# Seven half-size output products in three chunks of batches two and three

## The chip, the core and the metric

The kernel runs on one core of a Trainium2 chip. Its time is the device time of one execution in microseconds: before the change the median of three runs is 566.68 us, the lowest 566.61 and the highest 567.18. The profile is of one further execution, whose span is 564.8 us; times inside it count from the start of that span. TensorE (PE) multiplies matrices, VectorE (DVE) and ScalarE (ACT) work elementwise, GpSimd (POOL) issues the loads, and SyncE (SP) issues the stores and the transposing transfers. The clock granted to PE was full through the whole profile.

## The reference

Four batches of cross-covariance attention are followed by a feed-forward with a product of two projections. The attention matrix is 256 by 256 per batch, and it is made from sums over all 5824 rows; no nonlinear step follows the first product.

```python
def _attn_ref(q, k, v, tau):                         # q, k, v: (4, 5824, 256)
    qn = q / (np.linalg.norm(q, axis=1, keepdims=True) + 1e-06)
    kn = k / (np.linalg.norm(k, axis=1, keepdims=True) + 1e-06)
    s = kn.transpose(0, 2, 1) @ qn / tau             # (4, 256, 256)
    s = s - s.max(-1, keepdims=True)
    a = np.exp(s)
    a /= a.sum(-1, keepdims=True) + 1e-09
    return (v @ a).astype(np.float32)

def _moe_ref(x, w1, w2, w3, w_out):                  # x: (23296, 256), w1, w2: (256, 1024)
    a = x @ w1
    b = x @ w2
    h = a * b @ w3                                   # w3: (1024, 1024)
    return (h @ w_out).astype(np.float32)            # w_out: (1024, 256)
```

## The kernel before

The kernel never forms the attention output. It folds each batch's 256 by 256 attention matrix into the two projection weights (Wf), and it multiplies w3 by w_out once (W_sb). What is left per row is two projections of v, their elementwise product, and one output product of 1024 by 256.

A batch is cut into 12 chunks of rows: eleven of 512 rows and a last one of 192 columns (128 rows, and the 64 left over, which are handled for two batches together). A chunk has eight slots, one for each 128 of the 1024 features. A slot is the unit of the schedule: it makes the two projections into two PSUM banks, lets ACT cast the first to SBUF, and lets DVE multiply it by the second, straight from PSUM. There are four such banks, used in turn, so that a bank is wanted again two slots later. The evictions of the folds use the same four.

```python
    def bank(tag):
        if tag == "out":
            return {"tag": "out", "bufs": 3}
        turns[0] += 1
        return {"tag": f"ab{turns[0] % 4}", "bufs": 1}

    def emit_ab(b, c, j):
        n = chunk_cols(c)
        tiles = []
        for w in range(2):
            t = psum.tile([P, 512], F32, name=f"{'ab'[w]}_{b}_{c}_{j}", **bank("ab"))
            for ct in range(CT):
                nc.tensor.matmul(t[:, :n], lhsT=Wf[b][:, ct, w, j * P : (j + 1) * P], rhs=rhs_of(b, c, ct),
                                 start=(ct == 0), stop=(ct == CT - 1))
            tiles.append(t)
        a_sb = work.tile([P, 512], BF16, tag="a_sb", name=f"as_{b}_{c}_{j}", bufs=4)
        nc.scalar.copy(a_sb[:, :n], tiles[0][:, :n])
        # ... the last chunk: the same into left, with 192 columns
            ab = halves[j // 4][:, j % 4, :]
            nc.vector.tensor_mul(ab, a_sb, tiles[1])
        # ...
        if not seven(b, c):
            pend.append((slot[0] + LAG, 1, lambda only=None: emit_out(b, c, j, ab, only)))
        elif j == FT - 1:
            fns = seven_products(b, c, *halves)
            fns[0]()
            pend.extend((slot[0] + 1, 2, fn) for fn in fns[1:])
```

The output of a plain chunk is four matmuls of 256 columns in each slot (`emit_out`), two slots behind the projections, and two copies of 512 columns at the end, one on ACT and one on DVE. In batch four, and only there, the chunks but the last two take another way: the output product of the chunk, seen as 2 by 2 blocks, is made of seven products of half size and not of eight. That costs four sums on DVE for the left sides (s1 to s4), seven products of eight matmuls with 128 columns each, four copies of 256 columns on ACT and three additions of 256 columns on DVE. The right sides are prepared once, from W_sb, at the start of batch two (`combine_weights`: four differences on DVE and two casts on ACT). The seven products need the whole chunk, so that they are made in the slots of the next one, one product in each slot.

```python
    def seven(b, c):
        return b == B - 1 and c < NCH - 2

        # in seven_products:
        def p1():
            st["o"] = work.tile([P, 4, D], F32, tag="o_sb", name=f"osb_{b}_{c}", bufs=3)
            nc.vector.tensor_sub(s2, s1, a11)
            product("A", a11, w1, True)
            keep(0, 0)                               # ACT copies A to SBUF
        def p5():
            nc.vector.tensor_sub(s3, a11, a21)
            product("C", s1, t1, True)
        def p6():
            product("A", s2, t2)                     # adds onto A in the same bank
            keep(0, 1)
        # ... p7, p2, p4, p3 in the same manner
        return [sum1, p1, p5, p6, p7, p2, p4, p3]
```

While a batch runs, the scores of the next are made in the gaps: for each pair of rows, a G pair of matmuls and a square on ACT for the first row with q and another for the second with k, then one addition of the squares on DVE (1024 columns in fp32). After the scores comes a chain (norms, exponentials, sums), and then eight folds. All of this is placed by an agenda: each entry has a time on a clock that the emission of matmuls advances.

```python
        units = score_units(n)                       # 23 pairs x 3 units
        for i, (cst, fn) in enumerate(units):
            at(t0 + (t1 - t0) * i / len(units), cst, fn)      # t0, t1 = 16.0, 98.0 in batches two and three
        soft = soft_units(n)
        for cst, t, fn in soft:
            at(t1 + 1.0 + t, cst, fn)                # t: 0 (norms) ... 14.6 (sums), 15.6 + 1.1 * i (fold i)
    # ...
    for b in range(B):
        make_agenda(b)
        for c in range(NCH):
            for j in range(FT):
                run_due()
                emit_ab(b, c, j)
                room = 2
                while w_ready[0] and len(pend) > lag and pend[0][0] <= slot[0] and pend[0][1] <= room:
                    _, size, fn = pend.pop(0)
                    fn()
                    room -= size
                    run_due()
        run_due(1e9)
```

A plain output matmul group has size 1 and one of the seven products size 2, so that a slot holds at most two groups or one product.

Of the kernel before, what the change touches and what calls it, by code (L numbers as in the profile page):

```python
# [13 lines left out]
BF16 = DT.bfloat16  # L14

P = 128
# [9 lines left out]
def kernel(  # L26
# [12 lines left out]
    nc = tc.nc  # L39

    B, N, C = q.shape
# [9 lines left out]
    FT = F // P  # L51
# [6 lines left out]
    NCH = NT // 4 + 1  # L58
# [9 lines left out]
    work = ctx.enter_context(tc.tile_pool(name="work", bufs=2))  # L68
# [111 lines left out]
    def score_units(n):  # L180

        units = []
        npair = (NT + 1) // 2

        def pair_unit(pr, part):
            i0 = 2 * pr
            pi, o = divmod(i0, PIECE)
            qt, kt = pieces["q", n, pi], pieces["k", n, pi]
            if pr == 0 and part == 0:
                G_tiles[n] = psum.tile([P, CT, C], F32, tag="G", name=f"G_{n}", bufs=1)  # L190
                accs[n] = work.tile([P, 2, 2, C], F32, tag="acc", name=f"acc_{n}", bufs=1)
            G = G_tiles[n]
            if part < 2:
                if part == 0 and pr > 0:
                    sqs[0] = work.tile([P, 2, 2, C], F32, tag="sq", name=f"sq_{n}_{pr}", bufs=2)
                dst = accs[n] if pr == 0 else sqs[0]
                src = qt if part == 0 else kt
                nc.scalar.activation(out=dst[:, :, part, :], in_=src[:, o : o + 2, :], func=AF.Square)  # L198
                i = o + part
                for ct in range(CT):  # L200
                    nc.tensor.matmul(  # L201
                        G[:, ct, :],
                        lhsT=qt[:, i, ct * P : (ct + 1) * P],
                        rhs=kt[:, i, :],
                        start=(pr == 0 and part == 0 and ct == 0),
                        stop=(pr == npair - 1 and part == 1 and ct == CT - 1),
                        skip_group_check=True,
                    )
            elif pr > 0:
                nc.vector.tensor_add(accs[n], accs[n], sqs[0])  # L210

        sqs = [None]
        for pr in range(npair):
            for part in range(3):
                units.append((0.22 if part < 2 else 0.0, lambda pr=pr, part=part: pair_unit(pr, part)))
        return units
# [217 lines left out]
    clock = [0.0]  # L434
    agenda = []

    def run_due(upto=None):
        lim = clock[0] if upto is None else upto
        while agenda and agenda[0][0] <= lim:
            _, _, cost, fn = agenda.pop(0)  # L440
            clock[0] += cost
            fn()
# [3 lines left out]
    def at(t, cost, fn):  # L446
        seq[0] += 1
        agenda.append((t, seq[0], cost, fn))
# [17 lines left out]
    comb = {}  # L466

    def seven(b, c):
        return b == B - 1 and c < NCH - 2

    def combine_weights(step):

# [100 lines left out]
# [6 lines that stand above are left out]
                nc.tensor.matmul(  # L579
                    t[:, :n], lhsT=Wf[b][:, ct, w, j * P : (j + 1) * P], rhs=rhs_of(b, c, ct),  # L580
                    start=(ct == 0), stop=(ct == CT - 1),
                )
            tiles.append(t)
        a_sb = work.tile([P, 512], BF16, tag="a_sb", name=f"as_{b}_{c}_{j}", bufs=4)
        nc.scalar.copy(a_sb[:, :n], tiles[0][:, :n])  # L585
        if c == NCH - 1:
            if b % 2 == 0 and j == 0:
                lefts[b // 2] = work.tile([P, FT, 2, P + LEFT], BF16, tag="left", name=f"left_{b}", bufs=1)
            both = lefts[b // 2][:, j, b % 2, :]
            nc.vector.tensor_mul(both, a_sb[:, :n], tiles[1][:, :n])  # L590
            ab = both[:, :P] if b % 2 == 0 else both[:, LEFT:]
        else:
            if j % 4 == 0:
                halves[j // 4] = in_pool.tile([P, 4, 512], BF16, tag="big", name=f"abh_{b}_{c}_{j}", bufs=BIG_BUFS)
            ab = halves[j // 4][:, j % 4, :]
            nc.vector.tensor_mul(ab, a_sb, tiles[1])  # L596
        last_ab[0] = ab
        slot[0] += 1
        if not seven(b, c):
# [5 lines that stand above are left out]
        clock[0] += 4 * (n * MM_COL + MM_FIX)  # L605
# [55 lines left out]
    for nm in "kq":  # L661
        new_piece(nm, 0, 0)
        raw[nm] = work.tile([P, half, C], F32, tag="o_sb", name=f"raw_{nm}", bufs=3)
        first = nc.sync if nm == "k" else nc.scalar
# [101 lines left out]
        nc.gpsimd.partition_all_reduce(m, ones_f, P, ReduceOp.add)  # L766


    def make_agenda(b):
        agenda.clear()  # L770
        clock[0] = 0.0
        n = b + 1
        if b == 0:
            at(0.5, 0.87, soft0[5])
            for i in range(4):
                at((1.7, 2.6, 3.5, 3.9)[i], 0.43, soft0[7 + i])
            at(0.0, 0.0, load_library)
            at(4.6, 0.5, lambda: transpose_half_on_pe(0, 0, 1, False))
            at(7.0, 0.5, lambda: transpose_half_on_pe(0, 1, 0, True))
            at(8.0, 0.5, lambda: transpose_half_on_pe(0, 1, 1, False))  # L780
            at(15.0, 0.0, transpose_w3)
            at(15.0, 0.0, lambda: transpose_piece(0, 2))
            for jt in range(FT):
                at(27.5 + 1.2 * jt, 0.87, lambda jt=jt: w_unit(jt))
            moves = [("qk", 1, 0, 29.0), ("v", 0, 3, 30.0), ("v", 0, 4, 30.5), ("qk", 1, 1, 44.0), ("qk", 1, 2, 45.0)]
            moves += [("qk", 1, 3, 53.0), ("qk", 1, 4, 55.0), ("v", 0, 5, 61.0), ("qk", 1, 5, 73.0)]
            moves += [("v", 1, 0, 88.0), ("v", 1, 1, 98.0), ("v", 1, 2, 120.0), ("qk", 2, 0, 130.0)]
            t0, t1 = 54.0, 113.0
        else:
            moves = [("v", b, 3, 1.0), ("qk", n, 1, 10.0), ("qk", n, 2, 17.0), ("v", b, 4, 26.0), ("qk", n, 3, 38.0)]  # L790
            moves += [("v", b, 5, 46.0), ("qk", n, 4, 58.0), ("qk", n, 5, 66.0)]
            moves += [("v", n, 0, 76.0), ("v", n, 1, 86.0), ("v", n, 2, 96.0), ("qk", n + 1, 0, 108.0)]
            moves = [m for m in moves if m[1] < B]
            t0, t1 = 16.0, 98.0

        before = (0, 2) if b == 0 else None
        for nm, m, pi, t in moves:
            if before is not None and not (nm == "v" and before == (m, pi - 1) == (0, 3)):
                at(t, 0.0, lambda w=before: hold(vTs[w[0]][1][:1, 0, :1] if w[1] == NP_ - 1 else vTs[w[0]][0][:1, w[1] * PIECE, 0, :1]))
            at(t, 0.0, gate)  # L800
            if nm == "qk":
                at(t, 0.0, lambda m=m, pi=pi: load_qk(m, pi))
                before = None
            else:
                at(t, 0.0, lambda m=m, pi=pi: load_piece("v", m, pi))
                at(t + 4.0, 0.0, lambda m=m, pi=pi: transpose_piece(m, pi))
                before = (m, pi)
        if b == 1:
            for i in range(4):
                at(3.0 + 2.6 * i, 0.0, lambda i=i: combine_weights(i))  # L810
        if n == B:
            agenda.sort()
            return
        units = score_units(n)
        for i, (cst, fn) in enumerate(units):
            at(t0 + (t1 - t0) * i / len(units), cst, fn)
        soft = soft_units(n)
        for cst, t, fn in soft:
            at(t1 + 1.0 + t, cst, fn)
        agenda.sort()  # L820

    for b in range(B):
        make_agenda(b)
        for c in range(NCH):
            for j in range(FT):
                run_due()
                emit_ab(b, c, j)
                lag = 0
                if b == B - 1 and c >= NCH - 2:
                    lag = LAG_END if c == NCH - 1 else LAG + (LAG_END - LAG) * (j + 1) // FT  # L830
# [8 lines that stand above are left out]
    n = len(pend)  # L839
# [37 lines left out]
```

## Time and profile before

| What | Before |
|---|---|
| time, median of three | 566.68 us |
| span of the profiled run | 564.8 us |
| batch one, two, three, four start at about | 37, 180, 313, 445 us |
| DVE busy in 185 to 295 us (batch two) | 84.5 of 110 us |
| ACT busy there | 77.3 of 110 us |
| DVE busy in 453.1 to 553 us (batch four, seven products) | 86.8 of 99.9 us |
| ACT busy there | 61.5 of 99.9 us |

In the lines of the profile, L596 is the product of the projections on DVE, L585 the cast of the first projection, L579 the matmuls of both, L626 the plain output, L510 the seven products, L210 the addition of the squares, L198 the squares themselves, L201 the matmuls of the scores, L647 and L648 the output copies and L370 the folds. A line of a group gives the operation, its tiles and shape, how often it ran, its busy time and mean length, and the idle time before it with what ended it. A line of a timeline gives start, length, engine and what ran; the x at its end is the number of instructions merged into it. The length of a matmul includes the time in which the next one already runs, so that its cost is read from start to start.

### The profile page before, as it was taken

How to read it: one execution, taken by the hardware profiler on the slowest of the kernel's cores; microseconds unless marked ns; L12 is line 12 of the kernel's file. 1: busy time of each engine (PE TensorE's matmuls, PEld its weight loads, DVE VectorE, ACT ScalarE, POOL GpSimd, SP SyncE). 2: the span in 40 equal slices, each digit the busy share in tenths (PEclk: the TensorE clock that was granted, in tenths of full speed). 3: DMA queues.
4: the chain of work that ended last, by engine and by line, in shares of the span. 5: the costliest groups of instructions: out<-in, count | busy, mean ns of one | idle time of the engine just before them, and what ended most of it. 6: DMA issues, size and time to landing. Idle time of an engine off the chain costs nothing.

```text
span 564.8 us, 10684 instructions
## 1 busy us (share of the span) xinstructions
PE 553.4 (98%) x3988; PEld 355.3 (63%) x3995; DVE 403.5 (71%) x645; ACT 348.7 (62%) x659; POOL 78.3 (14%) x163
## 2 busy tenths in 40 slices
PE   7799999999999999999999999999999999999997
PEld 5764576776656666666656666666655666666665
DVE  1047645888967777888766567878876688888884
ACT  1047535777766577777665577777766666665663
POOL 4260013120120110120120010112020000100000
PEclk9999999999999999999999999999999999999999
DMA  9999989968455696685761586766650233440102
GB/s 214 211 181 209 171 175 230 226 169 198 112 150 113 112 215 148 110 158 146 151 152 43 133 180 157 137 132 122 158 152 38 67 93 79 98 102 38 75 39 95
DMA packets 75108, 77.50 MB, mean 137 GB/s; under 512 B 54192, under 2 KB 58800, under 8 KB 75056
## 3 DMA queue, kind: packets, MB, share of 16 engines
q0 software_dynamic: 15760, 38.93, 39.6%
q1 hardware_dynamic: 59008, 37.23, 22.5%
q10 hardware_dynamic: 288, 0.66, 0.4%
q8 instruction: 31, 0.51, 0.4%
q14 instruction: 21, 0.17, 0.1%
HBM read 78.91 MB, written 23.86 MB: 182 GB/s over the span
## 4 chain that ended last, share of the span: by engine, by line
PE 92%; DMA 5%; ACT 1%; DVE 1%; POOL 0%; issue 0%; DVEq 0%; ACTq 0%; POOLq 0%
PE b L579 28%; PE a L579 28%; PE o L626 22%; PE G L201 5%; DMA k<-in_k_dram 5%; PE prodA L510 3%; PE fold L370 2%; PE prodC L510 2%; PE w L752 1%; PE prodB L510 1%; ACT kr L292 0%; DVE Wf L379 0%; PE quarter L394 0%; POOL k L120 0%; POOL q L120 0%
## 5 line engine op out<-in xcount | busy, mean ns | idle before, releaser
L596 DVE TENSOR_TENSOR abh<-as,b 128x512 bf16<-128x512 bf16 x352 | 240.6, 685 | 116.1 <-ACT as L585 109.7
L585 ACT CAST as<-a 128x512 bf16<-128x512 f32 (+1 forms) x384 | 215.9, 562 | 146.1 <-PE a L579 94.7
L579 PEld LDWEIGHTS <-Wf 128*128 128x128 bf16 x1536 | 146.1, 98 | 103.8 <-issue 1.4
L579 PE MATMUL a<-vT,Wf 128*128 128x512 bf16 x704 | 209.4, 379 | 0.5 <-ACT Wf L403 0.4
L579 PE MATMUL b<-vT,Wf 128*128 128x512 bf16 x704 | 209.4, 379 | 0.0
L626 PE MATMUL o<-W_sb,abh 128*128 128x256 bf16 x1088 | 161.4, 273 | 0.0
L626 PEld LDWEIGHTS <-abh 128*128 128x128 bf16 x1088 | 106.3, 98 | 61.1 <-issue 0.2
L210 DVE TENSOR_TENSOR acc<-acc,sq 128x1024 f32<-128x1024 f32 x66 | 80.4, 1218 | 0.6 <-ACT sq L198 0.6
L201 PE MATMUL G<-k,q 128*128 128x256 bf16 x276 | 49.8, 273 | 0.0
L198 ACT ACTIVATE sq<-q 128x512 f32<-128x512 bf16 x66 | 41.8, 633 | 0.0
L198 ACT ACTIVATE sq<-k 128x512 f32<-128x512 bf16 x66 | 41.5, 629 | 0.0
L567 POOL COPY gate_t<-abh 1x1 bf16<-1x1 bf16 x39 | 10.5, 269 | 170.1 <-DVE abh L596 167.7
L201 PEld LDWEIGHTS <-q 128*128 128x128 bf16 x276 | 27.0, 98 | 3.1
L510 PEld LDWEIGHTS <-comb_S 128*128 128x128 bf16 x320 | 21.2, 98 | 9.4
L571 POOL COPY gate_t<-vT 1x1 bf16<-1x1 bf16 x16 | 2.9, 184 | 161.6 <-DMA vT<-v 161.6
L648 DVE COPY osb<-o 128x512 f32<-128x512 f32 x34 | 23.3, 684 | 0.9 <-PE o L626 0.9
L520 ACT COPY osb<-prodA 128x256 f32<-128x256 f32 x40 | 14.9, 372 | 11.7 <-PE prodA L510 11.7
L647 ACT COPY osb<-o 128x512 f32<-128x512 f32 x34 | 19.9, 586 | 3.5 <-PE o L626 2.1
L510 PEld LDWEIGHTS <-abh 128*128 128x128 bf16 x240 | 15.9, 98 | 7.1
L257 DVE TENSOR_TENSOR dk<-sqk,ident 128x256 f32<-128x256 f32 x1 | 0.4, 424 | 23.8 <-PE sqk L234 23.8
L377 ACT ACTIVATE Wf<-fold,rs 128x512 bf16<-128x512 f32 x15 | 10.3, 687 | 11.3 <-PE fold L370 8.1
L120 POOL DMA_DIRECT2D q<-in_q_dram x28 | 15.1, 541 | 12.7 <-DMA k<-in_k_dram 5.7
(116 smaller groups left out, 338.7 us busy)
## 6 DMA issues: line engine op xcount, KB each, us to landing
out_dram<-osb SPq DMA_DIRECT2D x44, 512.0 KB, 3.1
k<-in_k_dram POOLq DMA_DIRECT2D x19, 512.0 KB, 8.5
v<-in_v_dram POOLq DMA_DIRECT2D x19, 512.0 KB, 5.3
q<-in_q_dram POOLq DMA_DIRECT2D x18, 512.0 KB, 6.1
w_wout<-in_moe_w_dram POOLq DMA_DIRECT2D x1, 2048.0 KB, 23.0
k<-in_k_dram POOLq DMA_DIRECT2D x4, 320.0 KB, 8.2
v<-in_v_dram POOLq DMA_DIRECT2D x4, 320.0 KB, 5.0
q<-in_q_dram POOLq DMA_DIRECT2D x3, 320.0 KB, 4.2
```

The costliest lines, as they stand in the source:

```text
L120: nc.gpsimd.dma_start(out=pieces[nm, n, pi][:, lo:hi, :], in_=qk_main[nm, n][0][:, pi * PIECE + lo : pi * PIECE + hi, :])
L198: nc.scalar.activation(out=dst[:, :, part, :], in_=src[:, o : o + 2, :], func=AF.Square)
L201: nc.tensor.matmul(G[:, ct, :], lhsT=qt[:, i, ct * P : (ct + 1) * P], rhs=kt[:, i, :], start=(pr == 0 and part == 0 and ct == 0), stop=(pr ...
L210: nc.vector.tensor_add(accs[n], accs[n], sqs[0])
L510: nc.tensor.matmul(st[nm][:, i, :], lhsT=a[:, j, i * P : (i + 1) * P], rhs=w[j], start=(first and j == 0 and i == 0), stop=(j == 3), skip_ ...
L520: nc.scalar.copy(quarter(r, d), st["A"])
L579: nc.tensor.matmul(t[:, :n], lhsT=Wf[b][:, ct, w, j * P : (j + 1) * P], rhs=rhs_of(b, c, ct), start=(ct == 0), stop=(ct == CT - 1),)
L585: nc.scalar.copy(a_sb[:, :n], tiles[0][:, :n])
L596: nc.vector.tensor_mul(ab, a_sb, tiles[1])
L626: nc.tensor.matmul(tl[h][:, o, :], lhsT=lhsT, rhs=W_sb[:, j, :], start=(j == 0 and o == 0), stop=(j == FT - 1 and (small or o == 1)), skip ...
L647: nc.scalar.copy(o[:, 0:2, :], tl[0])
L648: nc.vector.tensor_copy(o[:, 2:4, :], tl[1])
```

## The change

Three of the eleven full chunks of batches two and three (indices 0, 3 and 6) take the seven half-size products too, which need fewer matmul columns: 7 x 8 x 128 and not 8 x 4 x 256 per chunk. Because the elementwise engines then have more to do in the chunk that follows (1, 4 or 7), two things lighten it there. The scores get a weight of 0.3 per slot in these chunks and 1.0 elsewhere, and are tied to slots 3 to 72 of the batch and not to the clock. And in slots 0, 2 and 4 of these chunks ACT casts the second projection as well, so that DVE multiplies two bf16 tiles of SBUF. The chain after the scores starts at slot 73, and the first two loads in the list are reordered, because the scores start earlier.

```diff
     def seven(b, c):
-        return b == B - 1 and c < NCH - 2
+        return c < NCH - 2 if b == B - 1 else b > 0 and c in (0, 3, 6)
+
+    def both_cast(b, c, j):
+        return 0 < b < B - 1 and c > 0 and seven(b, c - 1) and j in (0, 2, 4)
+
+    def scores_of(b, c):
+        return 0.3 if c > 0 and seven(b, c - 1) else 1.0
 # ... in emit_ab:
         nc.scalar.copy(a_sb[:, :n], tiles[0][:, :n])
+        right = tiles[1]
+        if both_cast(b, c, j):
+            right = work.tile([P, 512], BF16, tag="b_sb", name=f"bs_{b}_{c}_{j}", bufs=2)
+            nc.scalar.copy(right, tiles[1])
 # ...
-            nc.vector.tensor_mul(ab, a_sb, tiles[1])
+            nc.vector.tensor_mul(ab, a_sb, right)
 # ... in make_agenda, batches two to four:
-            moves = [("v", b, 3, 1.0), ("qk", n, 1, 10.0), ("qk", n, 2, 17.0), ("v", b, 4, 26.0), ("qk", n, 3, 38.0)]
+            moves = [("qk", n, 1, 1.0), ("v", b, 3, 8.0), ("qk", n, 2, 17.0), ("v", b, 4, 26.0), ("qk", n, 3, 38.0)]
 # ...
-            t0, t1 = 16.0, 98.0
+            t0, t1 = None, None
 # ...
+        if b > 0:
+            weights = [scores_of(b, s // FT) for s in range(SLOT0, SLOT1)]      # 3, 73
+            whole_ = sum(weights)
+            done = 0.0
+            for s, w in zip(range(SLOT0, SLOT1), weights):
+                first = -(-len(units) * done // whole_)
+                done += w
+                last = -(-len(units) * done // whole_) if s < SLOT1 - 1 else len(units)
+                by_slot.append((s, units[int(first) : int(last)]))
+
+            def chain():
+                for cst, t, fn in soft:
+                    at(clock[0] + 1.0 + t, cst, fn)
+                agenda.sort()
+
+            by_slot.append((SLOT1, [(0.0, chain)]))
+            agenda.sort()
+            return
 # ... in the loop over slots, ahead of emit_ab:
+                if b > 0:
+                    scores_due(c * FT + j)
```

More of the change, by code (lines that the diff above doesn't have):

```diff
@@ L766, in load_library, with scores_due @@
         nc.gpsimd.partition_all_reduce(m, ones_f, P, ReduceOp.add)
+    SLOT0, SLOT1 = 3, 73
+    by_slot = []
+    def scores_due(slot_):
+        while by_slot and by_slot[0][0] <= slot_:
+            for cst, fn in by_slot.pop(0)[1]:
+                clock[0] += cst
+                fn()
     def make_agenda(b):
@@ L814, in make_agenda @@
         units = score_units(n)
+        soft = soft_units(n)
+        if b > 0:
[14 more added lines that the diff above has]
+            return
         for i, (cst, fn) in enumerate(units):
             at(t0 + (t1 - t0) * i / len(units), cst, fn)
-        soft = soft_units(n)
         for cst, t, fn in soft:
```

## The prediction

> **What bounds the kernel now.** I read the page's busy times and slices first, then the chain that ended last, then the costliest groups, and then the timeline of a few stretches: a plain slot, one in which VectorE (DVE) is late, and one that already has seven products.
>
> ```profile
> PE 553.4 (98%) x3988; PEld 355.3 (63%) x3995; DVE 403.5 (71%) x645; ACT 348.7 (62%) x659; POOL 78.3 (14%) x163
> PE   7799999999999999999999999999999999999997
> ...
> PE 92%; DMA 5%; ACT 1%; DVE 1%; POOL 0%; issue 0%; DVEq 0%; ACTq 0%; POOLq 0%
> ...
> L596 DVE TENSOR_TENSOR abh<-as,b 128x512 bf16<-128x512 bf16 x352 | 240.6, 685 | 116.1 <-ACT as L585 109.7
> L585 ACT CAST as<-a 128x512 bf16<-128x512 f32 (+1 forms) x384 | 215.9, 562 | 146.1 <-PE a L579 94.7
> ...
> L210 DVE TENSOR_TENSOR acc<-acc,sq 128x1024 f32<-128x1024 f32 x66 | 80.4, 1218 | 0.6 <-ACT sq L198 0.6
> ```
>
> TensorE (PE) has no idle slice from the third to the last but one, and 92% of the chain is PE. Asked who waits in 185 to 300 us (all of batch two but its two ends), the waits of PE are empty. So these batches last as long as their matmuls, and every PE stall that the change brings is added in full.
>
> A plain slot, from the PE timeline (start, length, line):
>
> ```profile
> 283.38 0.59 PE L579 MATMUL a<-vT,Wf 128*128 128x512 bf16 x2
> 283.82 0.59 PE L579 MATMUL b<-vT,Wf 128*128 128x512 bf16 x2
> 284.25 0.60 PE L626 MATMUL o<-W_sb,abh 128*128 128x256 bf16 x4
> 284.68 0.59 PE L579 MATMUL a<-vT,Wf 128*128 128x512 bf16 x2
> ```
>
> From start to start: the a pair 0.43, the b pair 0.43, four output matmuls 0.43; a slot is 1.30 us, a chunk of eight 10.40.
>
> A slot in which DVE is late:
>
> ```profile
> 228.30 0.59 PE L579 MATMUL b<-vT,Wf 128*128 128x512 bf16 x2
> ...
> 228.43 0.68 DVE L648 COPY osb<-o 128x512 f32<-128x512 f32 x1
> 228.50 0.58 ACT L585 CAST as<-a 128x512 bf16<-128x512 f32 x1
> ...
> 229.03 1.22 DVE L210 TENSOR_TENSOR acc<-acc,sq 128x1024 f32<-128x1024 f32 x1
> 229.17 0.38 PE L201 MATMUL G<-k,q 128*128 128x256 bf16 x2
> ...
> 230.16 0.68 DVE L596 TENSOR_TENSOR abh<-as,b 128x512 bf16<-128x512 bf16 x1
> ```
>
> The b pair ends at 228.89, but its product with a starts at 230.16, behind a copy and an addition of squares, where it usually starts 0.22 after b's end. Next starts come 0.60 after the copy and 1.13 after the addition. PE did not notice: the bank of this b is wanted again two slots later. In a plain slot the reserve is 1.1 us: two slots of 1.30, less b's own 0.59, 0.22 to the product and its 0.69. Here it was 0.5: the product ended at 230.84 and the b that takes its bank started at 231.34. That reserve is what the change spends. Where it is gone already, at the small slots of batch three's end, the timeline shows it:
>
> ```profile
> 443.47 0.32 PE L579 MATMUL b<-vTt,Wf 128*128 128x192 bf16 x2 [0.18 <-DVE left L590]
> ```
>
> **What the skill says.** PSUM — Partial Sum Buffer, section Engine vs sequencer instructions: the VectorE and ScalarE queues are strict FIFO and matmuls start in program order. The trace agrees: the product above sits out 0.60 + 1.13 us behind the other two. Perfetto Trace Analysis, Optimizing Scalar/DVE Operations: the profiled length of an instruction is longer than the time it holds the engine, as its write acknowledgement overlaps the next. Here: 0.68 profiled, 0.60 from start to start; I use the latter for load and the former for when a result is there. VectorE: DVE Perf Modes, the perf-mode tier table: tensor_tensor runs 2x for bf16 in SBUF and 1x with any PSUM operand. Here: 512 elements with b in PSUM take 685 ns, 1024 bf16 elements of SBUF 684, and one 512-element bf16 sum of the combined weights 418. So casting b first takes a product from 685 to about 418 ns. Perfetto Trace Analysis, Optimization Strategy: repeated gaps on the engine that should be saturated can mean too few buffers. Before shows none; that is the form I expect of the loss.
>
> **The change, part by part.**
>
> *Products.* In batch four a chunk with seven products takes 453.12 to 463.15 on PE's timeline (first product to first product), 10.03 us against 10.40. Six chunks: 6 x 0.37 = 2.2 us less PE work. Nothing else of PE's work changes, so 564.5 is the floor.
>
> *Where PE's work goes.* The output matmuls of a seven chunk run in the next chunk (one product of 0.45 per slot). Its own slots 2 to 7 therefore hold a, b and scores alone. The scores keep their full rate there, since the 0.3 holds for the chunk after: 69 units (23 pairs of rows, each two parts with a G pair and a square, and one addition) over a weight of 46 x 1 + 24 x 0.3 = 53.2, so 1.3 units a slot, 0.87 parts and 0.43 additions. A G pair is 0.22 us (229.17 to 229.39), so PE has 0.87 + 0.87 x 0.22 = 1.05 us per slot, where it was 1.49 with the outputs. DVE's load there: 0.60 + 0.43 x 1.13 = 1.09, six slots 6.5, and 0.60 for the output copy of the chunk before: 7.1 us against PE's 6.4. The reserve shrinks too, by up to two output quartets (0.87 us), partly given back by scores.
>
> *Chunk index 3, in program order.* Zero is the start of a in slot 1. With no wait PE would start b in slots 4, 5, 6, 7 and in slot 0 of the next chunk at 3.90, 4.98, 6.06, 7.14, 8.01. DVE: product 1 from 1.25 (cast done) to 1.86, output copy to 2.46, addition to 3.59, product 2 to 4.20, visible 4.28. b of slot 4 needs product 2's bank: it starts at 4.33, a stall of 0.43. Product 3 to 4.80, addition to 5.94, product 4 to 6.54, visible 6.62: b of slot 6, now due 6.49, starts 6.67, 0.18. Product 5 to 7.15, addition to 8.28, product 6 to 8.89, visible 8.97: b of the next chunk, due 8.62, waits 0.40. Sum 1.0 us.
> *Chunk index 6.* The last addition falls one product later; the third wait goes. 0.6 us.
> *Chunk index 0.* Scores start in slot 3 and there is no copy of 512 columns, so only the wait at the next chunk's b remains: 0.3 us in batch three. In batch two two sums of the combined weights (685 ns each) lie in the same slots: 0.9 us.
> Stalls: 2 x (1.0 + 0.6) + 0.9 + 0.3 = 4.4 us.
>
> *The chunk after.* DVE: five products of 0.60, three of 0.34, four sums 0.60, three joins 0.34, one addition 1.13: 8.6 us of about 10.5. ACT: eleven casts at 0.48 (228.50 to 228.98), four copies at 0.27 (372 ns less 0.10), two squares at 0.53: 7.4 us. Both fit; the b casts cost ACT 1.4 us that lies beside PE.
>
> *The end of a batch.* The scores now end at slot 73, and the chain after them has fixed offsets. The eight folds move from slots 80-84 to slots 85-90, into the short slots of the last chunk, where the reserve before was 0.2 to 0.3 us (and 0.18 of stall at 443.47). Each fold takes a bank from the same four, and its eviction (687 ns on ACT, 745 on DVE) stands in the queue before a short product. Counted in the same way: the last two evictions hold an a for about 0.2 and a b for 0.5 us. 0.7 to 0.8 us at each of two ends, 1.5.
>
> *Loads.* The gates were reordered so that the score inputs still land early: a q and k pair took 5 to 10 us to land, and each is issued ten slots or more before its first use. No time.
>
> Sum: 566.7 - 2.2 + 4.4 + 1.5 = 570.4. Two roundings of mine lean to the slow side (a full 0.05 us from a result to the matmul that waits for it, and the fold evictions always in the worst order), so I say 569.8.
>
> **Rivals.**
> *The stalls are absorbed.* For it: DVE is 77% busy in 185 to 295 us, and batch four runs no-output slots without a stall. Against it: there each slot holds one product and no addition. If true, 564.5 to 565.5.
> *ACT becomes the bound.* In the seven chunk ACT's load is 0.48 + 0.87 x 0.53 = 0.94 of 1.05 per slot, and in the chunk after a b cast can push a copy of product A past the start of the next A product. It adds at most some 0.1 us per chunk: 571.
> *DVE falls further behind.* If a late product also delays the first sum and with it product C, each of six chunks loses another 0.6: 574.
> *A load comes late* and PE waits in the scores. Against it the landings above; 572 or more if it happens.
>
> **Range and chances.** The gain is known within 0.2 us; the loss is 3 to 8 us by the same bookkeeping, less if queues are more even than I draw them. I give 566.4 to 572.4. 2% is 11.3 us: faster by it is impossible below the floor, slower by it needs two rivals at once.
>
> **What would show it.** Right: the a, b and product starts of a whole seven-chunk cycle at 10.03 plus stalls; PE waits for DVE abh of 0.2 to 0.5 us each, two or three in chunks 3 and 6; one at the next chunk's first b after chunk 0, longer in batch two; waits for a fold's eviction at two batch ends; eighteen products fewer of 685 ns and eighteen of about 418; PE's busy matmul work 2.2 us less. Wrong: PE waits empty in batches two and three (then the time is under 565.5), or long waits on ACT casts or on DMA.

## The result, and the profile after

The changed kernel takes 570.33 us (median; 569.95 to 571.56) beside 566.64 us of the kernel before in the same comparison: 1.0067 times the time, interval 1.0049 to 1.0084. The profiled span grew from 564.8 to 568.5 us, by 3.7 us. The prediction was 569.8 us, its range 566.4 to 572.4, and its sum before rounding 570.4.

From the page of the kernel after, first the busy times, the slices of PE and the shares of the chain that ended last, and then two of the costliest groups (busy time, mean ns of one, then the idle time before it):

```profile
PE 556.4 (98%) x4139; PEld 356.2 (63%) x4139; DVE 415.0 (73%) x681; ACT 362.0 (64%) x695; POOL 82.3 (14%) x163
...
PE   8899999999999999999999999999999999999997
...
PE 87%; DMA 5%; DVE 3%; issue 2%; ACT 1%; POOL 0%; ACTq 0%; DVEq 0%; POOLq 0%
...
L607 DVE TENSOR_TENSOR abh<-as,b 128x512 bf16<-128x512 bf16 x334 | 227.6, 686 | 105.3 <-ACT as L592 96.1
...
L586 PE MATMUL b<-vT,Wf 128*128 128x512 bf16 x704 | 209.4, 379 | 2.7 <-DVE abh L607 2.5
```

The slices still look full, and PE's busy time even rose, by 3.0 us. It isn't more matmul work. Of the 3.0 us, 2.4 lie in the first 37 us (32.75 us busy there and 30.39 before), which the change does not touch; and after them a stall counts as busy as far as it lies under the recorded length of the matmul before it. The telling lines are the share of DVE in the chain, from 1% to 3%, and the last group: PE now waits before b for the product of DVE, 2.5 us in all. The same view with shapes apart has the 18 products that read two bf16 tiles:

```profile
L607 DVE TENSOR_TENSOR abh<-as,bs 128x512 bf16<-128x512 bf16 x18 | 7.6, 422 | 1.7 <-ACT bs L596 1.6
```

Each took 422 ns and not 686. They did what they were meant to; the experiments show that the time did not depend on it.

Asked for the waits of PE between 170 and 450 us (batches two and three), the kernel before answers

```profile
PE b L579 <- DVE left L590: 0.2, 1, 0.2
```

and the kernel after (total, times, longest, us)

```profile
PE b L586 <- DVE abh L607: 2.5, 7, 0.8
PE b L586 <- DVE Wf L379: 0.7, 2, 0.3
```

Seven new waits for a product and two for the eviction of a fold. These figures understate the loss. A pair of b should start 0.43 us after the pair of a. In chunk index 0 of batch two (start, length, what ran, idle before it and its releaser):

```profile
188.91 0.59 PE L586 MATMUL a<-vT,Wf 128*128 128x512 bf16 x2
190.29 0.59 PE L586 MATMUL b<-vT,Wf 128*128 128x512 bf16 x2 [0.78 <-DVE abh L607]
```

b starts 1.38 us after a, 0.94 too late, where the view says 0.78: the first 0.16 us are hidden under the recorded end of a. I therefore count all stalls from start to start, as the prediction did; a stall of less than 0.16 us shows no wait at all.

How such a stall comes about is seen in chunk index 3 of batch two (DVE's lines, and the last two of PE's):

```profile
217.86 0.69 DVE L607 TENSOR_TENSOR abh<-as,b 128x512 bf16<-128x512 bf16 x1 [0.62 <-PE o L637]
...
218.47 0.69 DVE L659 COPY osb<-o 128x512 f32<-128x512 f32 x1
...
219.06 1.22 DVE L210 TENSOR_TENSOR acc<-acc,sq 128x1024 f32<-128x1024 f32 x1
...
220.07 0.59 PE L586 MATMUL a<-vT,Wf 128*128 128x512 bf16 x2
...
220.20 1.28 DVE L607 TENSOR_TENSOR abh<-as,b 128x512 bf16<-128x512 bf16 x2
220.93 0.59 PE L586 MATMUL b<-vT,Wf 128*128 128x512 bf16 x2 [0.26 <-DVE abh L607]
```

Product 1, output copy, addition of squares and product 2 follow one another without a gap on DVE. Product 2 (the first of the two merged at 220.20) ends at about 220.89, and the b that takes its bank starts at 220.93, 0.86 after its a and so 0.43 late. That is the order and the size that the prediction wrote down for slot 4.

Where the 3.7 us are, from the starts of the first a of each batch: batch two went from 132.59 to 134.64 us, batch three from 132.14 to 133.48, together +3.4. The other 0.3 lie before the change has any effect (0.14 ahead of the first a, 0.16 in batch one). Kernels with the same batch one take 143.22 to 143.23 us for it (e1, e3, e4, e6) and not 143.38, so I count them as the scatter of one execution.

### The profile page after: what moved, and what is told of

It reads as the page before. It is cut to its first block, busy times and chain, and to the rows that moved or that the text cites. A ratio compares the mean times of both kernels' runs of the same rounds, so it can differ in the third digit from the quotient of the medians.

```text
span 568.5 us, 11030 instructions
## 1 busy us (share of the span) xinstructions
PE 556.4 (98%) x4139; PEld 356.2 (63%) x4139; DVE 415.0 (73%) x681; ACT 362.0 (64%) x695; POOL 82.3 (14%) x163
## 4 chain that ended last, share of the span: by engine, by line
PE 87%; DMA 5%; DVE 3%; issue 2%; ACT 1%; POOL 0%; ACTq 0%; DVEq 0%; POOLq 0%
PE b L586 26%; PE a L586 26%; PE o L637 18%; PE prodA L517 5%; DMA k<-in_k_dram 5%; PE G L201 5%; PE prodC L517 3%; PE fold L370 2%; DVE abh L607 2%; PE prodB L517 1%; PE w L763 1%; DVE acc L210 1%; DVE Wf L379 0%; DVE osb L659 0%; ACT kr L292 0%
## 5 line engine op out<-in xcount | busy, mean ns | idle before, releaser
L607 DVE TENSOR_TENSOR abh<-as,b 128x512 bf16<-128x512 bf16 x334 | 227.6, 686 | 105.3 <-ACT as L592 96.1
L637 PE MATMUL o<-W_sb,abh 128*128 128x256 bf16 x896 | 127.7, 273 | 0.0
L637 PEld LDWEIGHTS <-abh 128*128 128x128 bf16 x896 | 87.5, 98 | 42.2 <-issue 0.2
L517 PEld LDWEIGHTS <-comb_S 128*128 128x128 bf16 x512 | 33.8, 98 | 15.7 <-DVE comb_S L533 1.1
L574 POOL COPY gate_t<-abh 1x1 bf16<-1x1 bf16 x39 | 13.9, 357 | 166.6 <-DVE abh L607 166.0
L527 ACT COPY osb<-prodA 128x256 f32<-128x256 f32 x64 | 24.0, 375 | 15.2 <-PE prodA L517 15.2
L517 PEld LDWEIGHTS <-abh 128*128 128x128 bf16 x384 | 25.5, 98 | 11.3
L578 POOL COPY gate_t<-vT 1x1 bf16<-1x1 bf16 x16 | 4.7, 295 | 157.9 <-DMA vT<-v 157.9
L658 ACT COPY osb<-o 128x512 f32<-128x512 f32 x28 | 16.4, 586 | 5.9 <-PE o L637 5.1
L659 DVE COPY osb<-o 128x512 f32<-128x512 f32 x28 | 19.2, 687 | 0.9 <-PE o L637 0.9
L517 PE MATMUL prodA<-comb_T,comb_S 128*128 128x128 bf16 x256 | 19.5, 219 | 0.0
```

The costliest lines, as they stand in the source:

```text
L517: nc.tensor.matmul(st[nm][:, i, :], lhsT=a[:, j, i * P : (i + 1) * P], rhs=w[j], start=(first and j == 0 and i == 0), stop=(j == 3), skip_ ...
L527: nc.scalar.copy(quarter(r, d), st["A"])
L574: nc.gpsimd.tensor_copy(gate_t, last_ab[0][:1, :1])
L607: nc.vector.tensor_mul(ab, a_sb, right)
L637: nc.tensor.matmul(tl[h][:, o, :], lhsT=lhsT, rhs=W_sb[:, j, :], start=(j == 0 and o == 0), stop=(j == FT - 1 and (small or o == 1)), skip ...
L658: nc.scalar.copy(o[:, 0:2, :], tl[0])
```

## The experiments

The theory: PE stalls because DVE, in the chunks that have lost their own output matmuls, has products and additions of squares to do and PE has too little to do meanwhile; a smaller part is lost at the batches' ends. The rivals: ACT (the second casts), or the schedule of the scores as such. Unless said otherwise an experiment is the changed kernel with the edit shown.

**e1_quiet: no scores where PE is short.** The scores leave slots 2 to 7 of the chunks 0, 3 and 6 and lie in the other slots.

```diff
-    def scores_of(b, c):
+    def scores_of(b, c, j):
+        if seven(b, c) and j >= 2:
+            return 0.0
         return 0.3 if c > 0 and seven(b, c - 1) else 1.0
```

> The changed kernel with one thing different: the scores have weight 0 in slots 2 to 7 of the seven-product chunks themselves, where PE has no outputs; the 0.3 of the chunk after stays, and the plain chunks take the rest (1.9 units per slot). Theory (DVE is late in slots without outputs because additions of squares lie there, and PE then waits for the bank of a b): the 5.1 us of waits in chunks 0, 3, 6 and right after them nearly vanish, 565.5 us (565.0 to 566.5). Rival one (ACT, loaded by the casts of b, is what makes PE wait): those casts stay, 569.5 or more. Rival two (the folds in the short slots at the batch ends cost the time): they stay, 569.5 or more.

Measured: 566.57 us, 0.9997 of before (0.9989 to 1.0005). PE's waits in the same window:

```profile
PE b L588 <- DVE Wf L379: 0.7, 2, 0.3
PE b L588 <- DVE abh L609: 0.3, 2, 0.2
```

The loss of 3.7 us is gone with one condition, and the rivals (ACT, and the folds alone), which asked for 569.5 or more, fall. The time is 0.07 above the theory's range. From start to start 1.3 us of chunk waits are left, 0.67 of them in chunk index 6 of batch two.

**e2_no_additions: the suspected operation taken away.** The additions of squares of batches three and four (made during batches two and three) are left out, so that the norms there are those of the first pair alone. PE's and ACT's work stays.

```diff
-            elif pr > 0:
+            elif pr > 0 and n < 2:
```

> The changed kernel without the additions of squares in batches two and three (left out: the norms then come from the first pair of rows alone); squares, score matmuls and all casts stay where they are. Theory: DVE has 0.60 us per slot in the slots without outputs, so their waits go: 565.5 us (565.0 to 566.2). Rival one (ACT): ACT's work is the same, 569.5 or more. Rival two (folds at the ends): 569.5 or more.

Measured: 565.6 us, 0.9981 (0.9974 to 0.9988). No wait for a product is left:

```profile
PE b L586 <- DVE Wf L379: 0.7, 2, 0.3
```

At the same place of chunk index 3 the addition is missing, product 2 runs at once, and b follows a by 0.43:

```profile
219.23 0.69 DVE L607 TENSOR_TENSOR abh<-as,b 128x512 bf16<-128x512 bf16 x1
...
220.15 0.59 PE L586 MATMUL a<-vT,Wf 128*128 128x512 bf16 x2
...
220.58 0.59 PE L586 MATMUL b<-vT,Wf 128*128 128x512 bf16 x2
```

ACT has all its casts and squares in this kernel, and PE all its matmuls. So it is the additions in DVE's queue. The waits for the folds stay: they have another cause.

**e3_schedule_alone: the schedule without the products.** Seven products only in batch four as before; weights of 0.3 in chunks 1, 4 and 7, and the chain from slot 73, kept, and with it the later folds.

```diff
     def seven(b, c):
-        return c < NCH - 2 if b == B - 1 else b > 0 and c in (0, 3, 6)
+        return b == B - 1 and c < NCH - 2
     # ...
-        return 0.3 if c > 0 and seven(b, c - 1) else 1.0
+        return 0.3 if c in (1, 4, 7) else 1.0
```

> The changed kernel with seven products in batch four alone, as before, and one cast per slot; the scores keep their new places and weights (0.3 in chunks 1, 4 and 7), and so do the chain, the folds and the reordered loads. Theory: no slot lacks its outputs, so only the moved folds and the start are left, 567.2 us (566.8 to 567.7), plus 0.5 on before. If the moved folds cost the 1.5 us that were predicted: 568.2. If the new schedule is the loss: 569.5 or more.

Measured: 567.64 us, 1.0019 (1.001 to 1.0028). The two batches are 0.70 us longer than before (132.67 and 132.76 us), with waits at their ends alone:

```profile
PE b L586 <- DVE Wf L379: 0.7, 2, 0.3
PE b L586 <- DVE left L601: 0.2, 1, 0.2
```

So the moved folds cost their time without any new product (0.08 us in batch two, 0.62 in batch three), and the products with their stalls are the other 2.7 us (570.33 less 567.64).

**e4_one_cast: the second casts undone.** `j in (0, 2, 4)` becomes `j in ()`.

> The changed kernel with the second cast taken out: all products read b from PSUM. ACT loses 18 casts (1.4 us in each chunk after), DVE gets 0.27 us more in each of 18 products, 0.8 us in a chunk in which it was counted 8.6 of 10.5 us. Theory: nothing waits there, so 570.3, give or take 0.4. Rival one (ACT): faster, 569 or less. If the casts were needed: 571.5 or more.

Measured: 570.24 us, 1.0061 (1.0049 to 1.0074): no difference. In sum the casts neither cost nor bring anything. In batch two two small differences cancel: without the casts a b in chunk index 1, one of the chunks that they lighten, waits for 0.23 us, and the stall of 0.66 in slot 4 of chunk index 6 is 0.43.

**e5_weights_early: the four differences of the combined weights out of batch two.**

```diff
-        if b == 1:
+        if b == 0:
     # ...
-                at(3.0 + 2.6 * i, 0.0, lambda i=i: combine_weights(i))
+                at(116.0 + 3.0 * i, 0.0, lambda i=i: combine_weights(i))
```

> The changed kernel with one thing moved: the four differences and two casts of the combined weights are made late in batch one (after its scores), not in the first slots of batch two. Theory (their two 0.60 us DVE slots lie in front of the products of chunk 0): the wait of 0.94 us at the first b of chunk 1 in batch two falls to the 0.26 that batch three has, 569.7 us (569.3 to 570.0). Rival (that wait comes with the start of a batch, not with the sums): 570.3.

Measured: 570.33 us, 1.0057 (1.0044 to 1.007), a miss. In batch two the wait of chunk index 0 fell from 0.94 to 0.27 us as foreseen, and the batch by 0.68 (133.96). So the rival's figure of 570.3 was met, but not for its reason. In batch one a stall of 0.50 came up at the new place, and this execution also waited 0.9 us early in that batch for a load of v; batch one took 144.76 us where it takes 143.2 without the edit. The cost was moved, and the same stall is met again in e8 and e9.

**e6_even: no lighter chunk at all.** `scores_of` returns 1.0 everywhere.

> The changed kernel with the sparser scores undone: weight 1.0 in every slot, 0.99 units and not 1.3 in the slots without outputs, and 0.99 and not 0.39 in the chunk after. Theory (the additions in the slots without outputs are what hurts, and the chunk after has DVE time to spare: 7.5 us and 2.6 additions, 10.5 of 11.2): fewer waits in chunks 0, 3 and 6, about 2 of their 5 us gone, 568.5 us (567.6 to 569.3). Rival (the chunk after needs to be lightened): 571 or more.

Measured: 568.07 us, 1.0021 (1.0014 to 1.0028), 2.3 us less than the change. The lines between 170 and 450 us:

```profile
PE b L586 <- DVE abh L607: 1.1, 4, 0.3
PE b L586 <- DVE Wf L379: 0.7, 2, 0.3
PE prodA L517 <- DVE comb_S L537: 0.2, 1, 0.2
```

The weight of 0.3 lightens the chunk that runs the products, where the changed kernel waits only 0.22 us in each batch (product C of chunk 7), and for it raises the rate of scores in the chunk that is short of matmuls. Without it that chunk waits for 0.56 to 0.60 us in chunks 3 and 6 rather than 0.60 to 1.0, and product C of chunk 7 does not wait. One new wait appears in a chunk after, the first of batch two: two of its A products wait for the sums (0.32 and 0.17 from start to start, 0.6 us in that chunk with what follows from them). The lightening has a use, then, but in this one place alone.

**e7_all_three: everything that helped at once.** Scores left out of slots 1 to 7 of the seven chunks, 0.4 in the chunk after, the scores' end at slot 69, and the differences early as in e5.

```diff
+        if seven(b, c) and not (c > 0 and seven(b, c - 1)) and j >= 1:
+            return 0.0
-        return 0.3 if c > 0 and seven(b, c - 1) else 1.0
+        return 0.4 if c > 0 and seven(b, c - 1) else 1.0
     # ...
-    SLOT0, SLOT1 = 3, 73
+    SLOT0, SLOT1 = 3, 69
```

> Seven products where the change has them, and the scores kept out of slots 1 to 7 of those chunks (weight 0.4 in the chunk after, 1.0 elsewhere), the combined weights made in batch one, and the scores ended at slot 69, so that the folds come at slots 81 to 85 as before the change. Theory: the waits in the chunks and the moved folds both go, and the 2.2 us of saved matmul time come out less some 0.3: 564.8 us (564.3 to 565.6), which beats both kernels. Rival (the products themselves cost more than they save beside scores): 566.5 or more.

Measured: 574.13 us (570.99 to 575.25), 1.0116 (1.0095 to 1.0136), a clear miss. The waits for products are gone from batches two and three, and another stands in their place:

```profile
PE G L201 <- DMA k<-in_k_dram: 5.0, 2, 3.6
```

```profile
251.58 0.60 PE L201 MATMUL G<-k,q 128*128 128x256 bf16 x4 [3.56 <-DMA k<-in_k_dram]
```

That piece of k was issued at 242.32 us and landed at 251.54. With three quiet chunks the scores run denser elsewhere (2.1 units in a slot), and so they reach the fifth piece three to four slots earlier than its load was planned for.

**e8_pairs: seven chunks in pairs.** In the second chunk of a pair the products of the first fill PE, so that two chunks need but one quiet stretch. Eight seven chunks rather than six, and the scores' end at slot 71; the rest as in e7.

```diff
-        return c < NCH - 2 if b == B - 1 else b > 0 and c in (0, 3, 6)
+        return c < NCH - 2 if b == B - 1 else b > 0 and c in (0, 1, 4, 5)
```

> As the one with all three remedies, but the seven-product chunks stand in two pairs per batch (0, 1 and 4, 5), and the scores end at slot 71: the second of a pair has products in its slots, so that four chunks cost two stretches without outputs. Theory: PE work falls by 8 x 0.37 = 2.9 us, and DVE is at about 80% in the pairs: 564.2 us (563.6 to 565.2). Rival (three dense chunks in a row let DVE's lateness add up): 565.5 or more.

Measured: 564.7 us (564.14 to 566.01), 0.9963 (0.9951 to 0.9975): faster than both kernels. Batches two and three are 1.53 and 1.44 us shorter than before, 2.97 together, about the 8 x 0.37 that the prediction counted for chunks without stalls. Batch one took 143.7 us, 0.5 more, with e5's stall in it.

**e9_pairs_weights: the differences at other slots of batch one**, `115.2 + 1.3 * i`, to lose that stall.

> The pairs again, with the combined weights of batch one made at clock 115.2 to 119.1, before the steps of the chain that they ran into (a wait of 0.50 us at a b of batch one). Theory: that wait goes, 564.2 us (563.8 to 564.7). Rival (any place in batch one costs the same): 564.7.

Measured: 564.97 us, 0.9964 (0.995 to 0.9978), not told apart from e8. This is over the expected range. The stall stayed (0.50, and another of 0.19). Its timeline is in the last section.

**e10_three_load: e7 with the load of the fifth piece earlier**, ahead of one of v, and the differences as in e9.

```diff
-            moves += [("v", b, 5, 46.0), ("qk", n, 4, 58.0), ("qk", n, 5, 66.0)]
+            moves += [("qk", n, 4, 48.0), ("v", b, 5, 54.0), ("qk", n, 5, 66.0)]
```

> The one with all three remedies, with the fifth q and k pieces of the next batch loaded at clock 48 and not 58 (the sixth v piece after them, at 54), and the combined weights at 115.2 to 119.1. Theory (its slowness was one late load that the denser scores of chunk 5 ran into; all else was as foreseen): the waits of PE on k go, 564.8 us (564.3 to 565.5). Rival (dense scores themselves are slow): 568 or more.

Measured: 565.92 us, 0.9983 (0.9977 to 0.999). That is 8.2 us less than e7. Besides the two loads only the slots of the differences changed, and these made no difference from e8 to e9: the late k was e7's loss. The traced execution of e7, the fastest of its six, shows 5.0 of it. It is 0.4 above the expected range, with 0.68 us of stalls in batch one and 0.42 at the folds of each batch.

**e11_pairs_late: the pairs, with the differences left in batch two.**

> The pairs with the combined weights left in the first slots of batch two, as in the change; in these slots there are no additions of squares now. Theory (two sums of 0.60 us fit where the additions were taken out): the 0.50 to 0.68 us of waits in batch one go and at most 0.2 comes back in batch two, 564.3 us (563.9 to 564.8), the fastest of all. Rival (the sums cost half a microsecond wherever they stand): 564.8 or more.

Measured: 564.96 us (564.35 to 565.94), 0.9963 (0.9951 to 0.9976). The median is a little over the expected range. Batch one is back at 143.22 us, and batch two has two stalls of 0.17 and 0.16 instead. e8, e9 and e11 can't be told apart: wherever the four differences are made, they cost a few tenths.

**e12_three_late: e10 with the differences left in batch two.**

> The change's own chunks with scores kept out of them, folds at slots 81 to 85, the earlier load, and the combined weights left in batch two. Theory: 565.92 less 0.68 plus at most 0.2, 565.4 us (565.0 to 565.8), 1.3 below before, of which the matmuls' 2.2 are all and the rest are waits at the folds and in batch one. Rival: 565.9 or more.

Measured: 565.52 us, 0.9975 (0.9964 to 0.9986). Three single seven chunks gain too, 1.3 us of the 2.2, once neither scores nor a load stand against them; the pairs bring two chunks more for fewer quiet stretches.

## Why the prediction was right, and where its terms were off

The cause, most of the places and the size of the whole loss were those of the prediction; the shares were not. Its terms beside what the traces show, from start to start, both batches together:

| Term (us) | Predicted | Measured |
|---|---|---|
| less matmul work | -2.2 | -2.2 |
| chunk index 0, batch two and three | 0.9 and 0.3 | 0.94 and 0.26 |
| chunk index 3, slot 4, slot 6, next b | 0.43, 0.18, 0.40 | 0.43, 0.17, 0.39 |
| chunk index 6, batch two and three | 0.6 and 0.6 | 0.83 and 0.60 |
| product C in chunk 7 waits for the first sum | none | 0.22 and 0.22 |
| all chunk stalls | 4.4 | 5.05 |
| ends of the two batches | 1.5 | 0.55 net |
| scatter ahead of batch two | none | 0.3 |
| sum | 3.7 | 3.7 |

*The matmul gain* is seen by itself in e2, which has no chunk stall: its two batches are 1.69 us shorter than before (131.61 and 131.43), and it has 0.50 us more of stalls than before (0.45 at the ends, 0.05 at one b), which makes 2.19.

*The queue drawn by hand* for chunk index 3 held to 0.01 us at each of three waits, in both batches. Its cause is shown: without the additions the waits vanish (e2), without scores in those slots most do (e1). That it is its bank that a b waits for is read from the traces (it starts 0.04 us after the product that frees the bank has ended); no run changed the number of banks. The 0.23 us too little in chunk index 6 of batch two begin with the chunk's first product:

```profile
252.54 0.59 ACT L592 CAST as<-a 128x512 bf16<-128x512 f32 x1 [0.40 <-PE a L586]
...
253.40 0.69 DVE L607 TENSOR_TENSOR abh<-as,b 128x512 bf16<-128x512 bf16 x1 [0.85 <-PE o L637]
```

It starts 0.27 us after its cast has ended, behind an output matmul by the view, and copy, addition and product 2 after it are late by about as much. At the same place of batch three, and in e4, it follows its cast by 0.02 to 0.03 us. Why it is held there is open.

*The term that was mis-sized* is the end of a batch, 1.5 us. The waits there are 0.60 and 0.81 us, near the 0.7 to 0.8 predicted at each end; the longest of batch two is the b that was expected to wait for 0.5 us:

```profile
312.56 0.32 PE L586 MATMUL a<-vTt,Wf 128*128 128x192 bf16 x2
313.22 0.33 PE L586 MATMUL b<-vTt,Wf 128*128 128x192 bf16 x2 [0.34 <-DVE Wf L379]
```

The starts are 0.66 us apart, where the slot before has 0.17. But the prediction added them as if the kernel before had lost nothing from its fold stage to the batch's end. It had, 0.43 in each batch. In batch two a fold that follows four output matmuls is late:

```profile
298.64 0.60 PE L626 MATMUL o<-W_sb,abh 128*128 128x256 bf16 x4
299.33 1.02 PE L370 MATMUL fold<-w,e 128*128 128x512 bf16 x4
```

The starts are 0.69 us apart and not 0.43, a stall of 0.26, only 0.09 of it outside the recorded length. The rest of batch two's 0.43, and all of batch three's, lies at the short slots. Net of that the move of the folds costs 0.17 and 0.38 us. e3 bears out the sum and not the split: with the folds moved and no new products, the two batches are 0.70 us longer, but in batch three it has a stall of 0.32 where the changed kernel has 0.08. The prediction knew of the 0.18 us at 443.47 and did not subtract it.

*Of the rivals*, the absorbed stalls fell at once. ACT as the bound fell with e2, which leaves ACT's work as it is and loses the waits, and with e4: one cast fewer in three slots of a chunk did not change the time. "DVE falls further behind" happened in small: product C of chunk 7 waited, 0.22 us in each batch and not 0.6 in each of six chunks. From the PE timeline of the kernel after:

```profile
262.06 0.59 PE L586 MATMUL b<-vT,Wf 128*128 128x512 bf16 x2
262.71 0.62 PE L517 MATMUL prodC<-comb_T,comb_S 128*128 128x128 bf16 x8
```

C starts 0.65 us after b and not 0.43. *Loads* took no time in the change, as said; e7 shows that this held for that schedule only.

The total came out within 0.1 us of the hand sum by luck, because errors met: too little for the chunks (0.65), too much for the ends (0.95), and 0.3 of scatter. The 0.6 us taken off for roundings was wrong; those roundings lay in neither place.

## What to carry to other kernels

When output work moves into the next stretch, it is the stretch it left that becomes short of matmuls, and the elementwise work to lighten is there, not where the moved work lands. Count the reserve of the rotating banks from start to start, queue by queue, which gave the three stalls of chunk index 3 within 0.01 us, and subtract the stalls that the kernel before already has at the place something is moved from. Every denser schedule has to be read again against the landing times of its loads: a late piece in each of two batches cost more (8.2 us between e7 and e10) than the six seven chunks could bring (2.2).

## What the runs showed of the hardware

A difference of two SBUF tiles on DVE (128 x 512, fp32 out of bf16) took 685 ns in the kernel before. In e9 it lay beside GpSimd's reduction across partitions:

```profile
155.15 3.24 POOL L271 PARTITION_ALL_REDUCE tot<-acc  x1 [12.36 <-DVE acc L269]
155.60 0.68 DVE L661 COPY osb<-o 128x512 f32<-128x512 f32 x1
...
156.20 1.72 DVE L491 TENSOR_TENSOR comb_f<-W_sb 128x512 f32<-128x512 bf16 x1
...
158.58 0.59 PE L588 MATMUL b<-vT,Wf 128*128 128x512 bf16 x2 [0.33 <-DVE abh L609]
```

It took 1.72 us there, and 1722 to 1724 ns in each of the five kernels that place it so (e5, e7 to e10), while the copy out of PSUM under the same reduction kept its 0.68. The product behind it was late by about as much, and b waited. The Trainium skill, GPSIMD Engine Reference, section Specifications, says that GpSimd's SBUF interfaces are shared with VectorE, with contention for DVE instructions of two SBUF inputs. The two durations agree with that; no run moved the reduction alone, so that the cause is argued and not shown. On the size they say more than the page: the difference lost 1.04 us and was through at 157.92, before the reduction's recorded end at 158.39 (spans on GpSimd are rough).
